# Token division of a memory-augmented attention layer: sums as rows, inverted behind the memory's, spread through DRAM, outputs divided on GpSimd one segment later

## The chip, the cores and the metric

The kernel runs on one core of a Trainium2 chip. The metric is device time in microseconds for one launch; the kernel before takes 1630.69 us (median of 3 runs, 1630.55 to 1631.75). The engines are TensorE (PE; PEld is its weight load), VectorE (DVE), ScalarE (ACT), GpSimd (POOL) and SyncE (SP), which issues most DMAs. GpSimd cannot read PSUM, the memory that matmuls write to.

## What is computed

The input is 2048 rows of 512. Two layers alternate, twice: A, B, A, B, each added to its input after a layer norm. The change is in A, attention with a recurrent memory:

```python
for s in range(n_seg):                       # 64 segments of 32 tokens
    h = concatenate([mem, x[segment s]])     # 8 memory rows + 32 tokens
    q, k, v = h @ Wq, h @ Wk, h @ Wv         # 32 heads of 128
    p = softmax(where(mask, q @ k.T * scale, -1e9))
    o = (p @ v) @ Wo
    mem = o[:8]                              # goes into the next segment
    outs.append(o[8:])
```

The mask lets every row see the memory and each token the tokens up to itself. Only `mem` passes from segment to segment. B is a gated MLP over all rows (projection, gelu, layer norm, a 2048 x 2048 matmul across tokens, product, output projection).

## The kernel before, in words

All weights stay in SBUF. Each of the two A blocks runs 64 calls of `segment` (L891); `s` is the segment, `tb` a block of four segments (128 tokens), `j4` its number in the block. TensorE, VectorE and ScalarE run in the order of the program; GpSimd's and SP's order is chosen by the scheduler.

A segment computes Wo for the memory rows of its own segment together with the first 24 tokens of the segment before, so that 32 columns are full: `uT_cur` holds both, and the last 8 tokens of each segment (`oB`) are multiplied with Wo much later, in groups of four blocks (`y_part`). The order on TensorE is:

1. q and k for both halves of the heads (`qk`, L701: 16 matmuls of 512 columns, four at a time in column tiles; r is the half) and v for r = 0 (`v_mm`). ScalarE casts each result (L908), VectorE transposes it into QQ or KA (L911).
2. `scores(0)`, v for r = 1, `scores(1)`. ScalarE takes the exponent (`exps`, L943), VectorE multiplies by the mask into E (`close`, L946). Between the two `close` VectorE casts v (L1040).
3. `sums_ahead` (L969) gives the memory rows' softmax sums for r = 0; `pv(r)` (L986, L989) gives the unnormalised outputs in PSUM, psO[r]; `sums_memory` (L960) gives the memory rows' sums for r = 1; `sums_tokens` (L978) gives those of the token rows, on all 128 partitions at once because its weights are ones: 1024 numbers per partition in psT.
4. `memory_out(r)`: ScalarE inverts the memory's sums as exp(-ln) (L1003, L1004) and VectorE multiplies psO by them into uT_cur (L1005).
5. `wo_pairs` (L777, heads 0 to 17 into px) and `wo_rest` (L784, heads 18 to 31 into pw). `fold` (L873, L875, with ScalarE's copy `cross`, L1065) and `build_hA` (L882, L883) turn the result into the memory rows of hT, which the next segment's first matmul reads. `store_o` writes the 32 rows out through SP (L889).
6. ScalarE inverts all of psT (L1067, two L1070) into Rt, and VectorE divides the tokens: `tok_out` (L1008) into the next segment's uT, `last_out` (L1011) into oB, for r = 0 and 1.

At three points a `fill()` runs other TensorE work out of a generator: q, k and v of the last 8 tokens of the next blocks (`b_units`, six chunks of 16 matmuls of 0.86 us), or the Wo product of older oB rows (`y_part`). `b_units` hands out a chunk as 4 + 12 or 16 matmuls, so a segment takes 4, 12 and 16 at its three points: around `sums_ahead`, and at the end, while memT is built. Eight segments in all (j4 = 3 of the first four blocks of each A) have none. `run(copies)` casts the chunks on ScalarE; SP transposes them by DMA (L767). GpSimd copies, for a coming segment, the parts of QQ (L864) and KX (L867) that belong to other segments' last tokens (`prep_segment`).

Of the kernel before, what the change touches and what calls it, by code (L numbers as in the profile page):

```python
# [53 lines left out]
def _consts(ctx, tc, c, b_sp):  # L54
    nc = tc.nc
    cp = ctx.enter_context(tc.tile_pool(name="consts", bufs=1))
    bsp = cp.tile([P, 16], F32, name="bsp")
    tctx = ExitStack()
    tmp = tctx.enter_context(tc.tile_pool(name="consts_tmp", bufs=1))
    ident_f = tmp.tile([P, P], F32, name="ident_f")  # L60
    nc.gpsimd.memset(ident_f[:], 0.0)
    nc.gpsimd.affine_select(out=ident_f[:], in_=ident_f[:], compare_op=ALU.not_equal, fill=1.0,
                            base=0, pattern=[[-1, P]], channel_multiplier=1)
    ident_bf = cp.tile([P, P], BF16, name="ident_bf")
    nc.vector.tensor_copy(ident_bf[:], ident_f[:])


    maskf = tmp.tile([P, 224], F32, name="maskf")
    nc.gpsimd.memset(maskf[:], 1.0)
    fourth = tmp.tile([P, 4, 32], F32, name="fourth")  # L70
    nc.gpsimd.memset(fourth[:], 0.0)
    nc.gpsimd.affine_select(out=fourth[:], in_=fourth[:], compare_op=ALU.not_equal, fill=1.0,
                            base=0, pattern=[[-1, 4], [-4, 32]], channel_multiplier=1)
    own = maskf[:, 160:224].rearrange("p (i q) -> p i q", i=4)
    is_own = tmp.tile([P, 4, 1], F32, name="is_own")
    nc.vector.tensor_reduce(out=is_own[:], in_=fourth[:], op=ALU.max, axis=mybir.AxisListType.X)
    nc.vector.tensor_copy(own, is_own[:].to_broadcast([P, 4, 16]))
    for q in range(0, P, 32):
        blk = maskf[q:q + 32, 0:160].rearrange("p (i q) -> p i q", i=4)[:, :, 8:32]
        nc.gpsimd.affine_select(out=blk, in_=blk, compare_op=ALU.is_ge, fill=0.0, base=8,  # L80
                                pattern=[[0, 4], [1, 24]], channel_multiplier=-1)
        last = own[q:q + 32, :, 8:16]
        nc.gpsimd.affine_select(out=last, in_=last, compare_op=ALU.is_ge, fill=0.0, base=0,
                                pattern=[[1, 4], [4, 8]], channel_multiplier=-1)
    maskN = cp.tile([P, 2, 224], BF16, name="maskN")
    nc.vector.memset(maskN[:], 0.0)
    for gs in range(4):
        nc.vector.tensor_copy(maskN[32 * gs:32 * gs + 32, gs % 2, :], maskf[32 * gs:32 * gs + 32, :])
    ones = cp.tile([P, P], BF16, name="ones")
    nc.vector.memset(ones[:], 1.0)  # L90
    half = cp.tile([P, 2, 32], BF16, name="half")
    nc.vector.memset(half[:], 0.0)
    for g in range(2):
        nc.vector.memset(half[64 * g:64 * g + 64, g, :], 1.0)
    bsp_bf = cp.tile([P, 16], BF16, name="bsp_bf")

    def load_bsp():
        nc.vector.memset(bsp_bf[:], 0.0)
        nc.sync.dma_start(bsp_bf[:], b_sp.rearrange("(t p) -> p t", p=P))
        return lambda: nc.vector.tensor_copy(bsp[:], bsp_bf[:])  # L100

    c["bsp"], c["load_bsp"] = bsp, load_bsp
    tctx.close()
    c.update(ident_bf=ident_bf, maskN=maskN, ones=ones, half=half)
    return c


# [374 lines left out]
def kernel(  # L482
# [30 lines left out]
    rp = ctx.enter_context(tc.tile_pool(name="rows", bufs=1))  # L513
    rows = _Rows(nc, rp, xd, xb_d, o_d, x_in)
    rows.vb_d = dram.tile([P, 8 * DH], BF16, name="vb_d")
    with tc.manual_schedule(engines=ORDERED):
        _act_table(nc)
        for tt in range(2):
            x = rp.tile([P, DM], F32, name="x0", tag=("ln_x", "y_x")[tt])[:, 0:DM // 2].bitcast(BF16)
            nc.sync.dma_start(x, x_in[tt * P:(tt + 1) * P, :])  # L520
            rows.xs[tt] = x
        m0 = rp.tile([2 * M, DM], BF16, name="m0", tag="y_o")
        nc.vector.memset(m0[:], 0.0)
        nc.sync.dma_start(m0[0:M, :], A_mem0.rearrange("b m d -> (b m) d"))
        rows.m0T = rp.tile([P, KT, 2 * M], BF16, name="m0T")
        nc.sync.dma_start_transpose(out=rows.m0T[:], in_=m0[:].rearrange("t (kt s) -> t kt s", s=P))
        wqkv, rest = a_open_qkv_weights(tc, ctx, A_Wq, A_Wk, A_Wv)
        c = {}
        _ln_consts(ctx, tc, c)
        MV, RS = c["MV"], c["RS"]  # L530
        for tt in range(2):
            _stats(nc, rp, rows.xs[tt], MV[0][:, tt, :])
            _rstd_act(nc, RS[0][:, tt:tt + 1], MV[0][:, tt, 1:2], c)
            rows.apply(tt, MV[0], RS[0], first=True)
        _consts(ctx, tc, c, B_b_sp)
        rest()
# [120 lines left out]
def a_block(tc, c, rows, front, MV_in, RS_in, MV_out, RS_out, ahead, wo, S, first):  # L657
# [1 line left out]
    NSEG = S // SEG  # L659
    NB = S // P  # L660
    scale = float(DH) ** -0.5
    maskN, ones, half = c["maskN"], c["ones"], c["half"]

    with ExitStack() as ctx:

# [10 lines left out]
            KTBr[i], QTBr[i] = (a.rearrange("p (r h k) -> p r h k", r=2, h=16) for a in v[2:])  # L676
        pers = ctx.enter_context(tc.tile_pool(name="a_pers", bufs=1))
        wk = ctx.enter_context(tc.tile_pool(name="a_work", bufs=2))
        vsp = ctx.enter_context(tc.tile_pool(name="a_vs", bufs=2))
        rowp = ctx.enter_context(tc.tile_pool(name="a_rows", bufs=4))  # L680
        segp = ctx.enter_context(tc.tile_pool(name="a_seg", bufs=2))
        acc_pool = ctx.enter_context(tc.tile_pool(name="a_ps_acc", bufs=1, space=PSUM))
# [26 lines left out]

        memT = [pers.tile([P, P], BF16, name=f"memT{i}") for i in range(2)]  # L710
        NKQ = 2
        KAr = [pers.tile([P, 2, 16, 32], BF16, name=f"KA{i}") for i in range(2)]
        QQr = [pers.tile([P, 2, 16, 40], BF16, name=f"QQ{i}") for i in range(NKQ)]
        KXr = [pers.tile([P, 4, 2, 32], BF16, name=f"KX{i}") for i in range(NKQ)]
        uT = [pers.tile([P, H, 32], BF16, name=f"uT{i}") for i in range(2)]
# [20 lines left out]
        def run(todo):  # L736
            while todo:
                todo.pop(0)()

        def b_units(tb, early=0):  # L740
# [3 lines left out]
            for k, j in enumerate(order):  # L744
                now = k < early
                ps = (accB if now and k % 2 and j != 5 else accA).tile([P, 512], F32, name="psb")[:]
                for kts in (((0,), (1, 2, 3)), ((0, 1, 2, 3),))[k % 2]:
                    mm_chunk(ps, lambda kt, cg: bs["hB"][:, kt, :],
                             lambda kt, cg: qk_rhs(w, j, kt, cg) if j < 4 and now else cols_rhs(w, j, kt, cg), kts)
                    if kts[-1] != KT - 1:  # L750
                        yield
# [48 lines left out]
        def y_part(G, q, last=False):  # L800
# [5 lines left out]
                parts = [[(groups[g], 8 * q + k) for g in range(4)] for k in range(8)]  # L806
            pwB = accA.tile([P, DM], F32, name="pwB")
            for k, _ in enumerate(wo_last(parts, pwB)):
                if k in (0, 3):
                    yield  # L810

            def add(lo, n, src):
# [43 lines left out]

        seg_state = {}
        oBs = {}

        def prep_segment(s, eng=nc.gpsimd):  # L860
            tb, j4 = s // 4, s % 4
# [29 lines left out]
        def segment(s, fill, spare1, spare2, spare3, tail, loads):  # L891
            tb, j4 = s // 4, s % 4
            st = seg_state.pop(s)
            QQ, KX, VX = st["QQ"], st["KX"], st["VX"]
            KA = KAr[s % 2]
            VA = vsp.tile([P, 2, 4, DH], BF16, name="VA")
            hA_cur = rows.hT[tb][:, :, 24 + 32 * j4:56 + 32 * j4]
            uT_cur, uT_nxt = uT[s % 2], uT[(s + 1) % 2]
# [73 lines left out]
            def sums_tokens(ps):  # L972

                for k in range(2):
                    for g in range(2):
# [2 lines left out]
                        nc.tensor.matmul(o[:, :, :, 24:32] if k else o, lhsT=ones[64 * g:64 * g + 64, :],  # L978
                                         rhs=e_own(e, 1) if k else e_all(e, 8, 40), start=(k == 0), stop=True, skip_group_check=True)

            def pv(r):

                for i in range(4):
# [17 lines left out]
            def memory_out(r, ps):  # L1001
                rm = Rm[:, r]
                nc.scalar.activation(out=rm, in_=ps, func=ACT.Ln)  # L1003
                nc.scalar.activation(out=rm, in_=rm, func=ACT.Exp, scale=-1.0)  # L1004
                nc.vector.tensor_tensor(out=hview(uT_cur[:], r, 24, 32), in0=oview(r, 0, 8), in1=rm.rearrange("p g (n q) -> p g n q", q=8), op=ALU.mult)  # L1005

            def tok_out(r):
                nc.vector.tensor_tensor(out=hview(uT_nxt[:], r, 0, 24), in0=oview(r, 8, 32), in1=rview(r, 0, 24), op=ALU.mult)  # L1008
# [45 lines left out]
            spare1(E)  # L1054
            pv(1)
            sums_memory(1, sums[1])
            sums_tokens(psT)
            memory_out(1, sums[1])
            run(copies)
            px = accB.tile([P, 512], F32, name="px")  # L1060
            wo_pairs(px, uT_cur)
# [1 line left out]
            wo_rest(pw, uT_cur)  # L1063
            cross = wk.tile([P, P], F32, name="cross", bufs=1)
            beside = nc.scalar.copy(cross[0:64, :], px[64:128, 128:256])  # L1065
            Rt = segp.tile([P, 2, 512], F32, name="Rt", tag="Rt", bufs=1)
            nc.scalar.activation(out=Rt[:], in_=psT[:], func=ACT.Ln)  # L1067
            for r in range(2):
                rt = Rt[:, :, 256 * r:256 * r + 256]
                nc.scalar.activation(out=rt, in_=rt, func=ACT.Exp, scale=-1.0)  # L1070
            run(turns)
            spare2()
            t1 = wk.tile([P, P], F32, name="t1", bufs=1)
# [3 lines left out]
            if s > 0:  # L1077
                store_o(s, pw, t1)
            spare3()
            tok_out(0)  # L1080
            last_out(0)
            fill()
            run(copies)
            tok_out(1)
            last_out(1)
            run(adds)
            run(turns)
            tail()
# [4 lines left out]
        if first:  # L1093
            for tb in range(2):
                ln_turn(tb, nc.scalar.copy)
            units, units1 = b_units(0, 6), b_units(1, 2)
            for gen in (units, units1, units):
                for _ in range(3):
                    next(gen)
                    run(turns)  # L1100
                    run(copies)
                run(turns)
        else:
            blk_state[0] = dict(KTB=KTBr[0], QTB=QTBr[0], VB=VBr[0], VX=wo.VX[0])
# [7 lines left out]
            rows.y_load(y, first, nc.gpsimd, rows.pool.tile([P, DM], F32, name="y_x")[:], o)()  # L1112

        def values(units):
            for n in (2, 1):
                for _ in range(n):
                    next(units)
                run(copies)
                yield
# [151 lines left out]
```

## Time and profile before

| | us |
|---|---|
| median of 3 runs | 1630.69 |
| the profiled execution: its span | 1630.2 |
| a usual segment, from its first psQ matmul to the next one's | 10.00 |
| the first A block's segments 0 to 63 start at | 33.0 to 680.2 |
| the second A block's segments start at | 839.4 to 1475.0 |
| granted TensorE clock, mean | 0.996 |

The profiled execution has no run time of its own beside its span; the span is 0.5 us under the median of the runs. The page gives for each engine its busy time and share; a group's line gives code line, engine, operation, tile written <- tiles read, shapes, count, busy time, mean ns of one, and the idle time before it with what ended it. A matmul group's duration in a timeline runs to its modelled end; the distance to the next start is what it costs TensorE. The two A blocks hold some 1310 us of the span (33 to 693 and 839 to 1489), B nearly all of the rest.

### The profile page before, as it was taken

What the parts mean: (1) busy time and instruction counts of PE and PEld (TensorE: products, weight loads), DVE (VectorE), ACT (ScalarE), POOL (GpSimd) and SP (SyncE); (2) the same over time, 40 slices, a digit from 0 to 9 for tenths busy, and PEclk for the clock granted to TensorE, in tenths of its full rate; (3) what the DMA queues carried; (4) which work ended last, traced back from release to release, by engine and by line L of the source; (5) the groups of instructions that cost most, each with busy time, mean ns of one, the idle gap of its engine ahead of it and who ended that gap; (6) DMA issues with size and microseconds to landing.
All of it is one profiled execution on the core that took longest, in us unless ns stands there. A gap on an engine that the chain in (4) does not pass through costs nothing.

```text
span 1630.2 us, 90461 instructions
## 1 busy us (share of the span) xinstructions
PE 1575.0 (97%) x40658; PEld 962.0 (59%) x40658; DVE 1211.3 (74%) x3179; ACT 1064.1 (65%) x2278; POOL 290.2 (18%) x604
## 2 busy tenths in 40 slices
PE   4899999999999999999999999999999999999999
PEld 1456665665566556566656566666655666664565
DVE  3677777778888888884467777777888788878622
ACT  2577777777777777661047777777777777775400
POOL 5111111111211221320011111111121112224000
PEclk9899999999999999999999999999999999999999
DMA  9322122223321334387951222121233123425697
GB/s 352 105 44 43 44 44 44 43 46 75 81 56 43 79 87 84 91 182 145 214 167 48 45 50 46 46 46 46 62 97 79 46 72 95 98 55 172 141 189 162
DMA packets 264748, 149.27 MB, mean 92 GB/s; under 512 B 198680, under 2 KB 240784, under 8 KB 264360
## 3 DMA queue, kind: packets, MB, share of 16 engines
q1 hardware_dynamic: 251128, 99.66, 28.4%
q0 software_dynamic: 13232, 43.82, 8.3%
q8 instruction: 319, 5.23, 1.4%
q14 instruction: 69, 0.57, 0.1%
HBM read 59.68 MB, written 37.19 MB: 59 GB/s over the span
## 4 chain that ended last, share of the span: by engine, by line
PE 54%; DVE 1%; ACT 1%; DMA 1%; issue 0%; SPq 0%; DVEq 0%
PE pg L392 9%; PE psQ L701 7%; PE psK L701 7%; PE psb L701 5%; PE pz L291 4%; PE px L777 4%; PE psV L701 3%; PE psm L701 3%; PE psO L784 3%; PE py L435 2%; PE psO L986 2%; PE pwB L796 1%; PE psT L978 1%; PE psS L934 1%; PE pw L1223 0%; PE psO L969 0%
## 5 line engine op out<-in xcount | busy, mean ns | idle before, releaser
L701 PEld LDWEIGHTS <-hT 128*32 128x32 bf16 x12288 | 331.9, 97 | 309.2 <-DVE hT L883 65.5
L911 DVE STREAM_TRANSPOSE QQ<-rows 128x512 bf16<-128x512 bf16 x256 | 179.2, 700 | 20.2 <-ACT rows L908 13.0
L911 DVE STREAM_TRANSPOSE KA<-rows 128x512 bf16<-128x512 bf16 x256 | 176.3, 689 | 14.7 <-ACT rows L908 13.1
L908 ACT CAST rows<-psQ 128x512 bf16<-128x512 f32 x256 | 142.8, 584 | 22.7 <-PE psQ L701 21.1
L392 PE MATMUL pg<-z,wspT 128*128 128x344 bf16 x1024 | 154.3, 309 | 0.0
L1005 DVE TENSOR_TENSOR uT<-psO,Rm 128x128 bf16<-128x128 f32 x256 | 74.5, 291 | 106.7 <-PE psO L989 56.6
L1070 ACT ACTIVATE Rt<-Rt 128x512 f32<-128x512 f32 x256 | 147.3, 622 | 4.1
L1008 DVE TENSOR_TENSOR uT<-psO,Rt 128x384 bf16<-128x384 f32 x256 | 140.4, 548 | 10.8 <-ACT Rt L1070 4.1
L701 PE MATMUL psQ<-Wq_sb,hT 128*32 128x512 bf16 x2048 | 136.2, 383 | 10.2 <-ACT Rt L1067 4.4
L943 ACT ACTIVATE S<-psS 128x224 bf16<-128x224 f32 x256 | 91.4, 357 | 81.1 <-PE psS L938 81.1
L777 PEld LDWEIGHTS <-uT 128*32 128x32 bf16 x4608 | 111.6, 96 | 46.8 <-DVE uT L1005 32.7
L701 PE MATMUL psQ<-Wk_sb,hT 128*32 128x512 bf16 x2048 | 136.2, 383 | 0.0
L777 PE MATMUL px<-Wo,uT 128*32 128x256 bf16 x3840 | 135.3, 275 | 0.3 <-DVE uT L1005 0.3
L701 PE MATMUL psm<-Wq_sb,hT 128*32 128x512 bf16 x2048 | 134.9, 380 | 0.0
L701 PE MATMUL psK<-Wk_sb,hT 128*32 128x512 bf16 x2048 | 134.4, 379 | 0.0
L701 PE MATMUL psK<-Wv_sb,hT 128*32 128x512 bf16 x2048 | 134.4, 379 | 0.0
L701 PE MATMUL psV<-Wv_sb,hT 128*32 128x512 bf16 x2048 | 133.6, 378 | 0.0
L1067 ACT ACTIVATE Rt<-psT 128x1024 f32<-128x1024 f32 x128 | 131.0, 1024 | 3.1
L784 PE MATMUL psO<-Wo_high,uT 128*32 128x128 bf16 x7168 | 126.9, 220 | 5.9 <-issue 3.3
L392 PEld LDWEIGHTS <-wspT 128*128 128x128 bf16 x1024 | 100.2, 98 | 53.2
L867 POOL COPY KX<-old 128x128 bf16<-128x128 bf16 x128 | 69.1, 550 | 299.3 <-PE psS L938 224.8
L867 POOL COPY KX<-front 128x128 bf16<-128x128 bf16 x126 | 66.6, 548 | 303.9 <-PE psS L938 222.5
(194 smaller groups left out, 2908.2 us busy)
## 6 DMA issues: line engine op xcount, KB each, us to landing
o_d<-o_sb SPq DMA_DIRECT2D x126, 64.0 KB
vb_d<-front SPq DMA_DIRECT2D x30, 256.0 KB
VX<-vb_d SPq DMA_DIRECT2D x120, 64.0 KB
ln_x<-xd SPq DMA_DIRECT2D x26, 256.0 KB
y_o<-o_d POOLq DMA_DIRECT2D x22, 256.0 KB, 3.4
xd<-y_o POOLq DMA_DIRECT2D x22, 256.0 KB, 3.2
Wq_sb<-in_A_Wq_dram POOLq DMA_DIRECT2D x8, 512.0 KB, 9.7
Wk_sb<-in_A_Wk_dram POOLq DMA_DIRECT2D x8, 512.0 KB, 11.1
```

The source lines that it names most:

```text
L392: nc.tensor.matmul(pg[t][:, k, 0:344], lhsT=wsp[t][:, st, :], rhs=z(st, 344 * k, 344 * k + 344), start=(st == 0), stop=(st == NT - 1))
L701: return [nc.tensor.matmul(ps[32 * cg:32 * cg + 32, :], lhsT=lhs(kt, cg), rhs=rhs(kt, cg), start=(kt == 0), stop=(kt == KT - 1), tile_posi ...
L777: nc.tensor.matmul(px[at:at + 32, 0:256], lhsT=lhs[:, h, :], rhs=wo_rhs(h, slice(k + 2, None, -2) if h % 2 else slice(k, None, 2)), start= ...
L784: nc.tensor.matmul(pw[32 * cg:32 * cg + 32, :], lhsT=lhs[:, h, :], rhs=wo_rhs(h, cg), start=False, stop=(h == H - 1), tile_position=(0, 32 ...
L867: eng.tensor_copy(KX[:, :, r].rearrange("p g (k i) -> p i g k", i=4), bs["KTB"][:, r].rearrange("p (i g) k -> p i g k", i=4)[:, :, :, 8 * ...
L908: return r, mms, nc.scalar.copy(r[:], ps)
L911: nc.vector.transpose(out=QQ[:, j % 2, :, 0:32] if j < 2 else KA[:, j % 2], in_=r[:])
L943: return nc.scalar.activation(out=S[:, r], in_=psS[:, r, 0:224], func=ACT.Exp, scale=scale)
L1005: nc.vector.tensor_tensor(out=hview(uT_cur[:], r, 24, 32), in0=oview(r, 0, 8), in1=rm.rearrange("p g (n q) -> p g n q", q=8), op=ALU.mult)
L1008: nc.vector.tensor_tensor(out=hview(uT_nxt[:], r, 0, 24), in0=oview(r, 8, 32), in1=rview(r, 0, 24), op=ALU.mult)
L1067: nc.scalar.activation(out=Rt[:], in_=psT[:], func=ACT.Ln)
L1070: nc.scalar.activation(out=rt, in_=rt, func=ACT.Exp, scale=-1.0)
```

## The change

`sums_rows` replaces `sums_tokens` in all segments but the last of each A. Its weights, `pick`, put the sums of 64 partitions on 16 equal rows, so that eight matmuls of at most 128 columns give all sums as 8 distinct rows, psT[:, 0, 0:128], instead of 1024 numbers on each partition. Right behind the memory's inversion ScalarE inverts these 128x128 numbers (Rr). SP writes the 8 distinct rows to DRAM (`r_d`, 4 KB) and reads them back four times with all 128 partitions as the target (Rt, 4 x 128 KB). The unnormalised outputs leave PSUM as copies into `raw` (f32): r = 1 by ScalarE behind `cross`, r = 0 by VectorE where `tok_out(0)` stood. Four GpSimd products of `raw` and Rt fill uT and oB; they are emitted in the next segment, behind its `sums_rows`. A fourth `fill()` stands ahead of the memory's second inversion, between the sums and `wo_pairs`, and the chunks are handed out as 4 + 8 + 4 and 16 matmuls. KA and VA become single buffers.

```diff
+    pick = cp.tile([P, 2, 16], BF16, name="pick")
+    nc.vector.memset(pick[:], 0.0)
+    for g in range(2):
+        nc.vector.memset(pick[64 * g:64 * g + 64, g, :], 1.0)
...
+    rows.r_d = [dram.tile([8, P], F32, name=f"r_d{i}") for i in range(2)]
...
-        vsp = ctx.enter_context(tc.tile_pool(name="a_vs", bufs=2))
+        vsp = ctx.enter_context(tc.tile_pool(name="a_vs", bufs=1))
...
-        KAr = [pers.tile([P, 2, 16, 32], BF16, name=f"KA{i}") for i in range(2)]
+        KAr = [pers.tile([P, 2, 16, 32], BF16, name="KA")]
...
-                for kts in (((0,), (1, 2, 3)), ((0, 1, 2, 3),))[k % 2]:
+                for kts in (((0,), (1, 2), (3,)), ((0, 1, 2, 3),))[k % 2]:
...
-                if k in (0, 3):
+                if k in (0, 2, 3):
                     yield
...
+            def sums_rows(ps):
+
+                for k in range(2):
+                    for q in range(4):
+                        e = E[:, q // 2, q % 2, :]
+                        rhs = e[:, 160:224].rearrange("p (i b e) -> p i b e", i=4, b=2)[:, :, 1, :] if k else heads40(e[:, 0:160])[:, :, 8:40]
+                        o = ps[32 * q:32 * q + 32, :].rearrange("p (i q) -> p i q", i=4)
+                        nc.tensor.matmul(o[:, :, 24:32] if k else o, lhsT=pick[:].rearrange("p g m -> p (g m)"), rhs=rhs,
+                                         start=(k == 0), stop=True, tile_position=(0, 32 * q), skip_group_check=True)
...
+            def raw_out(raw, r, copy):
+
+                copy(raw[:].rearrange("p (r g n) q -> p r g n q", r=2, g=2)[:, r], oview(r, 8, 40))
...
             sums_memory(1, sums[1])
-            sums_tokens(psT)
+            ahead_of = s + 1 < NSEG
+            if ahead_of:
+                sums_rows(psT[:, 0, 0:P])
+            else:
+                sums_tokens(psT)
+            if late:
+                late.pop(0)()
+            if not (first and s == 0):
+                fill()
             memory_out(1, sums[1])
+            Rt = segp.tile([P, 2, 512], F32, name="Rt", tag="Rt", bufs=1)
+            if ahead_of:
+                Rr = segp.tile([P, P], F32, name="Rr", bufs=1)
+                nc.scalar.activation(out=Rr[:], in_=psT[:, 0, 0:P], func=ACT.Ln)
+                nc.scalar.activation(out=Rr[:], in_=Rr[:], func=ACT.Exp, scale=-1.0)
+                r_d = rows.r_d[s % 2]
+                nc.sync.dma_start(r_d[:], Rr[:].rearrange("(a b) c -> a b c", b=16)[:, 0, :])
+                for q in range(4):
+                    nc.sync.dma_start(Rt[:, q // 2, :].rearrange("p (g s c) -> p g s c", g=2, s=2)[:, :, q % 2, :],
+                                      r_d[2 * q:2 * q + 2, :].partition_broadcast(P))
             run(copies)
...
-            nc.scalar.activation(out=Rt[:], in_=psT[:], func=ACT.Ln)
-            for r in range(2):
-                rt = Rt[:, :, 256 * r:256 * r + 256]
-                nc.scalar.activation(out=rt, in_=rt, func=ACT.Exp, scale=-1.0)
+            if ahead_of:
+                raw = segp.tile([P, H, 32], F32, name="raw", bufs=1)
+                raw_out(raw, 1, nc.scalar.copy)
+
+                def norm_tokens():
+
+                    rb = Rt[:].rearrange("p r (h q) -> p (r h) q", q=32)
+                    for o, lo, hi in ((uT_nxt[:, :, 0:24], 0, 24), (oB[:, :, 8 * (s % 16):8 * (s % 16) + 8], 24, 32)):
+                        for r in range(2):
+                            n = slice(16 * r, 16 * r + 16)
+                            nc.gpsimd.tensor_tensor(out=o[:, n], in0=raw[:, n, lo:hi], in1=rb[:, n, lo:hi], op=ALU.mult)
+
+                late.append(norm_tokens)
+            else:
...
-            tok_out(0)
-            last_out(0)
+            if ahead_of:
+                raw_out(raw, 0, nc.vector.tensor_copy)
+            else:
+                tok_out(0)
+                last_out(0)
             fill()
             run(copies)
-            tok_out(1)
-            last_out(1)
+            if not ahead_of:
+                tok_out(1)
+                last_out(1)
```

The last segment of each A keeps the old path. The start of the first A and its first segment hand out four parts in place of three.

## Prediction, on record before the run

> **What bounds the kernel now.** I read the page's shares, then the windows of single segments, then the timeline of one segment, then the DMA and GpSimd queues. Times inside a segment are counted from its first psQ matmul and written T+.
>
> ```profile
> PE 1575.0 (97%) x40658; PEld 962.0 (59%) x40658; DVE 1211.3 (74%) x3179; ACT 1064.1 (65%) x2278; POOL 290.2 (18%) x604
> ```
>
> TensorE looks full, but that does not say that its work sets the time. From one segment's first psQ matmul to the next one's, most of the 128 segments take 10.00 us, and a few take 9.80. The windows of one of each (length, then busy us and instructions of PE, PEld, DVE, ACT and POOL, granted clock, DMA share, GB/s):
>
> ```profile
> 1041.22:1051.22 10.00, 10.00 (x309) 5.99 (x308) 7.93 (x21) 7.55 (x17) 1.80 (x4) 1.00 0.15 38
> 910.90:920.70 9.80, 8.76 (x277) 5.36 (x273) 8.10 (x21) 7.28 (x17) 2.39 (x5) 1.00 0.20 43
> ```
>
> The second has no `fill` in it: 1.72 us less TensorE work (32 matmuls, 0.86 us per 16) buys only 0.20 us. So a chain through all engines takes 9.80 us, and a filled segment is 0.20 us of TensorE work above it. The end of that chain, in the unfilled segment:
>
> ```profile
> 917.05 0.38 DVE L946 TENSOR_TENSOR E<-S,maskN 128x448 bf16<-128x448 bf16 x1
> ...
> 917.49 0.32 PE L986 MATMUL psO<-E,VA 64*128 64x80 bf16 x8 [0.41 <-ACT Rm L1004]
> ...
> 917.70 0.22 PE L960 MATMUL psO<-E,ones 64*128 64x64 bf16 x4
> ...
> 917.75 0.44 PE L978 MATMUL psT<-E,ones 64*128 64x512 bf16 x4
> ...
> 917.99 0.28 ACT L1003 ACTIVATE Rm<-psO 128x128 f32<-128x128 f32 x1 [0.49 <-PE psO L960]
> ...
> 918.12 1.05 PE L777 MATMUL px<-Wo,uT 128*32 128x256 bf16 x30
> ...
> 918.64 0.29 DVE L1005 TENSOR_TENSOR uT<-psO,Rm 128x128 bf16<-128x128 f32 x1 [0.36 <-ACT Rm L1004]
> ...
> 918.90 0.39 PE L777 MATMUL px<-Wo_high,uT 128*32 128x256 bf16 x6
> ```
>
> The second E (E1, L946) ends at T+6.53, its pv at once follows, then the memory's sums, Ln, Exp, the product for heads 16 to 31 (done T+8.03), heads 16 and 17 of px, the rest, fold, memT, hT. L978, which the change removes, stands beside this chain: Ln starts without it, and heads 0 to 15 (32 matmuls, 0.85 us) end at T+8.07, just when the chain delivers.
>
> **What the change takes away.** TensorE loses L978's step (917.75 to 918.12, 0.37) and gets eight matmuls of 32 columns; sixteen such (L969) step 0.12, so 0.06 to 0.12, say 0.10. A quarter chunk of fill (0.215) moves from ahead of pv to ahead of px. A filled segment is then bound by the chain up to heads 16 (T+8.09), four more matmuls (0.11), the rest of Wo (step 0.78), and the last fill (0.86): 9.85. An unfilled one stays at 9.80, which is why I count nothing for TensorE there. 126 segments change, 8 are unfilled: 118 x 0.15 = **17.7 us**.
>
> VectorE drops two 0.55 (L1008) and two 0.28 (L1011) for one PSUM copy like L1040's 0.69. It lies after memT, beside the next segment's projections; the transposes behind it are then released by TensorE. Only segments now over 10.00 can gain; all their excess is 10.7 us, and I take 2.
>
> ScalarE drops 1.02 + 2 x 0.62 of Rt and gets Ln 0.28 and Exp 0.31 on 128x128 and one raw copy (0.58). The Ln and Exp now stand ahead of the chunk's cast and `cross`: after L1004 (start T+7.39) starts step 0.22, 0.31, 0.22, 0.51, so cross starts at T+8.65 instead of T+8.44. L875 then ends at T+9.23, while pw's last matmul lands at T+9.16: 0.01 to 0.05 late, inside the 9.85. If the cast took longer, each tenth would be on the chain.
>
> Sum so far: 1630.2 - 17.7 - 2 = **1610.5**.
>
> **What it adds: the division on GpSimd.** Per segment four products of two SBUF operands, 128x384 twice and 128x128 twice. The nearest row is L223 on GpSimd, 128x512 f32, 1.21; scaled 0.91, so 0.93. The floor is 0.60 (L864, 256 elements copied in 0.40, times 1.5), the ceiling 1.21. The small ones lie between hB's 0.30 and KX's 0.55: 0.42. The four take 2.7 us. GpSimd has 8 us spare per segment, so its sum costs nothing; its place does. The product for segment s is built into GpSimd's queue ahead of the KX and QQ copies that wait for the next scores, so it runs as soon as its Rt halves have landed.
>
> When is that? Exp of Rr ends at T+8.23. SP writes r_d; the nearest landings in the trace's events are o_d<-o_sb (64 KB, median 2.43, fastest 2.38) and xb_d (fastest 1.71, median 2.92): I take 2.1 for 4 KB. Only then do the four Rt loads go out, at the 0.45 spacing of VX's issues. A VX load of 64 KB lands in 1.8 to 3.6, median 2.87, behind a 256 KB write; for 128 KB with little ahead I take 2.4. The first half is there at 8.27 + 2.1 + 0.05 + 0.45 + 2.4 + 0.05 = 13.3, which is **T+3.5** of the next segment; the ends (1.7 and 1.8; 3.2 and 3.6) give T+2.5 to T+5.8. The second half follows 0.9 later. Where hT's transpose (1.20) and ln_x (0.58) are ahead of r_d on SP, which is every fourth segment, it is 1 us later. px needs the products at T+7.2 and T+8.1: they are done by T+5.8, so TensorE does not wait for GpSimd.
>
> By the Trainium skill, "DMA: Bandwidth & Descriptors", section "Anatomy of one DMA — SWDGE (gpsimd) path", a DMA costs about 2.0 us plus bytes over 436 GB/s; that is given for the other queue, and an estimate by it (2.0 and 2.3) puts the first half at T+3.3 and the sum at about 1657. The medians of the rows above are higher, so the trace does not agree.
>
> But the products then run exactly where VectorE multiplies S by the mask: E0 asks at T+5.12 and E1 at T+6.14, with VectorE's 0.69 cast between them without a gap. These two exclude GpSimd. In the trace a KX copy that begins 0.02 to 0.03 after E takes 0.685 instead of 0.477, and an E that begins just after a GpSimd copy takes longer by the copy's size: 0.49 behind 128 elements, 0.61 behind 256, against 0.38 alone. The second case and its GpSimd copies, from the timelines:
>
> ```profile
> 1127.63 0.61 DVE L946 TENSOR_TENSOR E<-S,maskN 128x448 bf16<-128x448 bf16 x1
> ```
>
> ```profile
> 1127.60 0.40 POOL L864 COPY QQ<-old 128x256 bf16<-128x256 bf16 x1 [0.81 <-PE psO L969]
> 1127.94 0.62 POOL L867 COPY KX<-old 128x128 bf16<-128x128 bf16 x1
> ```
>
> The block is about 0.9 ns per copied element; a product reads twice as much and takes 0.93, so I let it hold VectorE for 0.85. With the first half at T+3.5: products 3.50 to 4.43, 4.85, then the second large one 4.85 to 5.78; E0 asks at 5.12, runs at 5.70, 0.58 late, E1 and the chain as much. The delay is a sawtooth in the arrival: worked the same way, T+3.0, 3.25, 3.5, 3.75 and 4.0 give 0.10, 0.35, 0.60, 0.85 and 0.28, mean 0.44. Arrivals will scatter as the landings do; I take 0.40. 126 x 0.40 = **50 us**. The floor is nothing (arrival by T+2.5, or hits in a gap), the ceiling about 0.65 (the mean around T+4.4).
>
> The Trainium skill, "SBUF — State Buffer", section "SBUF: two separate sides", speaks against the change too: a VectorE operation with two SBUF inputs and a reading GpSimd operation lock each other out "for the whole instruction". The trace agrees that they exclude, not on the length: behind the whole 0.40 of QQ the E above would have taken 0.75, it took 0.61. An estimate by the rule makes each block some 0.1 longer and the sum about 1670.
>
> Sum: 1610.5 + 50 = 1660.5. The profiled span of 1630.2 stands 0.5 below the median of the runs, 1630.69, so **1661**.
>
> **The rest at nothing.** The Rt loads write 0.5 MB more per segment, 1024 packets of 512 B at the 29 ns of such packets, 1.9 us on 16 engines out of 10: hidden by engines that are 15 to 21% busy, else landings move later. SP's issues add 0.4 + 4 x 0.45 and a wait of 2; behind them stand o_d (its tile is rewritten 6 us later) and K's transposes (used a segment later). Single KA and VA buffers are rewritten at T+2.7 and T+5.0, after their readers of the segment before.
>
> **Rivals.**
> - *Faster, 1610 (0.26).* The products miss E: Rt lands by T+2.5, or a product holds VectorE much shorter than a copy's 0.9 ns per element lets expect. For it: the fastest landings just give that. Against: the medians, and the transposes in the same queue.
> - *No change, 1630 (0.08).* Hits cost 0.16 on average and eat the gain, or the cast on ScalarE does.
> - *Much slower, 1750 (0.04).* Landings of 4 us put the products behind T+6; px then waits for GpSimd. At T+6.0 the E delay is 0.7 and px waits 0.4: 126 x 1.1 on 1610.
> - That the scheduler queues this segment's KX copies behind the products, so that scores wait, is excluded by the built order: those copies serve the segment after next.
> - *My forecast, slower around 1661 (0.62),* its own range 1636 to 1690, turned by one mechanism: E behind a product on the shared port. It decides at a mean delay of 0.16.
>
> **How the numbers follow.** Faster 0.26; same 0.08; slower 0.62 + 0.04. A difference within 0.2% (1627.4 to 1634) cannot be told from none here. The range reaches from the fast rival, 1606, to the ceiling of 0.65 per segment, 1692.
>
> **What would show it.** Right: E's spans of 0.4 to 1.2 us with GpSimd products beside them; TensorE's idle time ended by E ahead of the second pv; filled segments of 10.1 to 10.6 us; the products starting at T+3 to T+4.5. Wrong: E at 0.39 throughout and filled segments at 9.85 (fast rival), or px's weights waiting for GpSimd's uT (late rival), or cross waiting for nothing but ScalarE with L875 the last to arrive (no change).

## The result, and the profile after

The changed kernel takes 1765.8 us (median of 4 runs, 1757.8 to 1774.0) against 1630.6 for the kernel before: 1.082 times as long, 95% interval 1.0774 to 1.0866. I had forecast 1661 and a range up to 1692: the change did lose, but by more than four times as much. The profiled execution has a span of 1770.0 us.

The page after, engines, then two of the DMA queues (packets, MB, share of 16 engines' span) and the chain that ended last:

```profile
PE 1612.5 (91%) x41139; PEld 981.4 (55%) x41162; DVE 1191.7 (67%) x2804; ACT 953.8 (54%) x2278; POOL 630.2 (36%) x1108
...
q1 hardware_dynamic: 390232, 166.27, 41.7%
...
q8 instruction: 323, 5.29, 1.3%
...
PE 65%; DMA 13%; DVE 9%; POOL 3%; issue 3%; ACT 3%; SPq 2%; POOLq 0%; DVEq 0%; ACTq 0%
```

The shares of PE, DVE and ACT all fell: the time has grown, and DVE and ACT have less work, part of which went to GpSimd (630.2 us busy, 290.2 before). Before, the chain was TensorE, with 1% of DMA and 1% of VectorE in it; now 13% is DMA and 9% VectorE. q1 carried 99.7 MB before (28.4%); what came on top, 66.6 MB, is the 126 writes of r_d with their Rt loads. q8 brings instructions, in packets of 16 KB (5.23 MB before); it will matter.

A segment takes 11.27 us on average in the first A and 11.03 in the second (10.08 and 10.07 before; the first two segments of each A are left out), about 1.1 us more in some 125 segments. Two of them show two ways to lose. Windows of both (length, busy us of the engines, clock, DMA):

```profile
1044.44:1054.95 10.51, 10.04 (x309) 5.97 (x309) 7.46 (x18) 6.44 (x16) 4.31 (x8) 1.00 0.34 87
999.92:1011.98 12.06, 10.26 (x310) 5.96 (x313) 7.04 (x18) 6.44 (x16) 4.10 (x8) 1.00 0.28 78
```

In the first, a product meets E (timeline):

```profile
1050.30 0.99 POOL L1114 TENSOR_TENSOR uT<-raw,Rt 128x384 bf16<-128x384 f32 x1 [5.43 <-DMA Rt<-r_d]
...
1050.59 0.95 DVE L952 TENSOR_TENSOR E<-S,maskN 128x448 bf16<-128x448 bf16 x1
...
1051.60 0.32 PE L1002 MATMUL psO<-E,VA 64*128 64x80 bf16 x8 [0.47 <-DVE E L952]
```

E takes 0.95 in place of 0.39 and the second pv waits for it, as forecast; but the product starts at T+5.9, not T+3.5. In the second segment Rt is later still. Its SP queue and GpSimd's products:

```profile
997.90 1.19 SPq L209 DMA_TRANSPOSE hT<-ln_xn  x1
999.14 0.57 SPq L198 DMA_DIRECT2D ln_x<-xd  x1
999.82 0.59 SPq L1093 DMA_DIRECT2D r_d<-Rr  x1
```

```profile
1003.20 2.89 SPq L1095 DMA_DIRECT2D Rt<-r_d  x4
...
1007.81 0.98 POOL L1114 TENSOR_TENSOR uT<-raw,Rt 128x384 bf16<-128x384 f32 x1 [5.57 <-DMA Rt<-r_d]
...
1008.85 1.05 PE L782 MATMUL px<-Wo,uT 128*32 128x256 bf16 x30 [1.50 <-POOL uT L1114]
...
1010.21 0.29 PE L782 MATMUL px<-Wo_high,uT 128*32 128x256 bf16 x4 [0.31 <-POOL uT L1114]
```

The write of r_d is issued behind hT and ln_x, 0.1 us before the segment starts, the loads follow 3.4 us later, the product runs at T+7.9, and px, for which TensorE stood idle from T+7.4, at T+8.9. E is undisturbed here. A third kind of loss has no partner in the segment at all: TensorE waits for nothing that the profile shows. The waits of TensorE's weight loads (us in total, times, longest):

```profile
PEld L782 <- POOL uT L1114: 56.6, 58, 5.1
PEld L1002 <- ACT Rm L1019: 48.2, 114, 0.4
PEld L1002 <- DVE E L952: 41.2, 75, 2.9
...
PEld L706 <- issue: 34.9, 81, 3.0
...
PEld L975 <- issue: 29.9, 52, 2.9
```

The wait for Rm (L1019) was there before (50.5). "issue" of all TensorE lines sums to 96.5 us of weight-load waits, 27.7 before.

### The profile page after: what moved, and what is told of

It is laid out like the page before. It is cut to its first block, busy times and chain, and to the rows that moved or that the text cites. A ratio compares the mean times of both kernels' runs of the same rounds, so it can differ in the third digit from the quotient of the medians.

```text
span 1770.0 us, 92820 instructions
## 1 busy us (share of the span) xinstructions
PE 1612.5 (91%) x41139; PEld 981.4 (55%) x41162; DVE 1191.7 (67%) x2804; ACT 953.8 (54%) x2278; POOL 630.2 (36%) x1108
## 4 chain that ended last, share of the span: by engine, by line
PE 65%; DMA 13%; DVE 9%; POOL 3%; issue 3%; ACT 3%; SPq 2%; POOLq 0%; DVEq 0%; ACTq 0%
PE psQ L706 11%; PE psK L706 10%; PE pg L396 8%; PE psb L706 6%; DMA Rt<-r_d 6%; PE px L782 5%; DVE E L952 5%; PE psO L789 5%; PE psm L706 5%; PE pz L295 4%; DMA r_d<-Rr 3%; POOL uT L1114 2%; PE psO L1002 2%; PE py L439 2%; DVE VA L1060 2%
## 5 line engine op out<-in xcount | busy, mean ns | idle before, releaser
L706 PEld LDWEIGHTS <-hT 128*32 128x32 bf16 x12288 | 336.1, 97 | 325.8 <-DVE hT L889 70.8
L1114 POOL TENSOR_TENSOR uT<-raw,Rt 128x384 bf16<-128x384 f32 x252 | 254.9, 1011 | 664.2 <-DMA Rt<-r_d 506.9
L914 ACT CAST rows<-psQ 128x512 bf16<-128x512 f32 x256 | 149.7, 585 | 137.6 <-PE psQ L706 137.6
L917 DVE STREAM_TRANSPOSE KA<-rows 128x512 bf16<-128x512 bf16 x256 | 181.8, 710 | 40.8 <-ACT rows L914 34.9
L782 PEld LDWEIGHTS <-uT 128*32 128x32 bf16 x4608 | 123.1, 97 | 86.4 <-POOL uT L1114 56.6
L952 DVE TENSOR_TENSOR E<-S,maskN 128x448 bf16<-128x448 bf16 x256 | 159.3, 622 | 15.2 <-POOL seen L1197 0.6
L706 PE MATMUL psQ<-Wq_sb,hT 128*32 128x512 bf16 x2048 | 140.5, 385 | 19.5 <-DVE hT L889 10.9
L789 PE MATMUL psO<-Wo_high,uT 128*32 128x128 bf16 x7168 | 133.4, 225 | 8.8 <-issue 6.7
L1019 ACT ACTIVATE Rm<-psO 128x128 f32<-128x128 f32 x256 | 71.1, 278 | 112.9 <-PE psO L966 92.2
L789 PEld LDWEIGHTS <-uT 128*32 128x32 bf16 x7168 | 120.0, 100 | 12.7 <-issue 11.7
L706 PE MATMUL psb<-Wq_sb,hB 128*32 128x512 bf16 x992 | 87.1, 391 | 21.3 <-ACT hB L629 16.8
```

Source lines behind the costliest of these rows:

```text
L706: return [nc.tensor.matmul(ps[32 * cg:32 * cg + 32, :], lhsT=lhs(kt, cg), rhs=rhs(kt, cg), start=(kt == 0), stop=(kt == KT - 1), tile_posi ...
L782: nc.tensor.matmul(px[at:at + 32, 0:256], lhsT=lhs[:, h, :], rhs=wo_rhs(h, slice(k + 2, None, -2) if h % 2 else slice(k, None, 2)), start= ...
L789: nc.tensor.matmul(pw[32 * cg:32 * cg + 32, :], lhsT=lhs[:, h, :], rhs=wo_rhs(h, cg), start=False, stop=(h == H - 1), tile_position=(0, 32 ...
L914: return r, mms, nc.scalar.copy(r[:], ps)
L917: nc.vector.transpose(out=QQ[:, j % 2, :, 0:32] if j < 2 else KA[:, j % 2], in_=r[:])
L952: nc.vector.tensor_tensor(out=E[:, r], in0=S[:, r].unsqueeze(1).to_broadcast([P, 2, 224]), in1=maskN[:], op=ALU.mult)
```

## The experiments

Theories at the start: **lateness** (the trips through DRAM end later than I reckoned; products meet E, and px waits), **traffic** (the transfers or SP's queue delay other work), **rearrangement** (the new order itself loses). The times, each with its ratio to runs of the kernel before on the same chip (four chips; the kernel before takes 1629.2 to 1630.9 on them); the last column sums the weight-load waits named issue:

| run | us | ratio, 95% interval | issue |
|---|---|---|---|
| before | 1630.6 | | 27.7 |
| no_trip | 1639.0 | 1.0031 to 1.0068 | 41.5 |
| cross_first | 1638.4 | 1.0039 to 1.0070 | 43.6 |
| trip_small | 1631.2 | 0.9998 to 1.0024 | 32.0 |
| trip_alone | 1683.8 | 1.0315 to 1.0367 | 75.9 |
| short_products | 1712.5 | 1.0475 to 1.0528 | 82.7 |
| changed kernel | 1765.8 | 1.0774 to 1.0866 | 96.5 |
| before_half | 1637.1 | 1.0030 to 1.0065 | 35.2 |
| before_one | 1655.6 | 1.0106 to 1.0183 | 52.1 |
| before_trip | 1674.8 | 1.0244 to 1.0298 | 68.4 |
| products_on_E | 1643.5 | 1.0056 to 1.0098 | |
| on_E | 1694.8 | 1.0370 to 1.0434 | 34.0 |
| behind_E | 1898.3 | 1.1571 to 1.1690 | 34.4 |
| one_load | 1722.9 | 1.0537 to 1.0606 | 86.8 |
| half_bytes | 1731.4 | 1.0598 to 1.0671 | 85.6 |
| one_load_ord | 1766.8 | 1.0815 to 1.0860 | 92.8 |
| half_bytes_ord | 1728.6 | 1.0558 to 1.0624 | 76.9 |

**The trip taken out, alone, and small.** no_trip drops the five DMAs:

```diff
-                nc.sync.dma_start(r_d[:], ...)
-                for q in range(4):
-                    nc.sync.dma_start(Rt[...], r_d[2 * q:2 * q + 2, :].partition_broadcast(P))
```

> Leaves out the write of r_d and the four Rt loads; Rt is filled once with ones, so the token outputs stay undivided. Lateness theory (the two trips through DRAM end later than I reckoned, so that the products meet E and px waits for them): nothing of the loss is left, products start before T+2, E takes 0.39, 1605 to 1620 us. Traffic theory (the transfers and SP's queue delay other work): the same, 1605 to 1620. Rearrangement theory (Rr's inversion ahead of cross, the sums as rows, the fourth fill, single KA and VA lose time themselves): still over 1640.

1639: nearly the whole loss is gone, but nothing is gained either; of that below. trip_alone keeps the DMAs and takes the products out:

```diff
-                            nc.gpsimd.tensor_tensor(out=o[:, n], in0=raw[:, n, lo:hi], in1=rb[:, n, lo:hi], op=ALU.mult)
+                            if lo:
+                                nc.gpsimd.memset(o[:, n], 0.5)
+                            else:
+                                nc.gpsimd.tensor_tensor(out=junk[:, n], in0=raw[:, n, 0], in1=rb[:, n, 0], op=ALU.mult)
```

> The write of r_d and the Rt loads stay, but the products of uT shrink to 16 elements per partition into a tile that nothing reads, and those of oB become a constant, so the token outputs are wrong. Nothing waits for Rt but GpSimd, and nothing long stands beside E. Lateness theory: 1605 to 1630 us, E at 0.39. Traffic theory: over 1700, as slow as the changed kernel or nearly. Rearrangement theory: over 1640.

1684: not what lateness gives, and less than I had given traffic. It stands 45 us above no_trip, which still has the long products, although no engine but GpSimd waits for Rt directly. trip_small tells whether SP's issues or the packets do this (its short products, too, cover 2 partitions only):

```diff
-                    nc.sync.dma_start(Rt[:, q // 2, :]..., r_d[2 * q:2 * q + 2, :].partition_broadcast(P))
+                    nc.sync.dma_start(Rt[0:2, q // 2, :]..., r_d[2 * q:2 * q + 2, :].partition_broadcast(2))
```

> As the run with the trip alone (nothing waits for Rt, no long products, token outputs wrong), but the four Rt loads fill 2 partitions in place of 128: the same five issues on SP and the same waits there, 1/64 of the bytes and packets. Traffic theory (the 1024 packets of the Rt loads keep the DMA engines from bringing TensorE's next block of instructions in time): the waits named issue fall back to some 50 us, 1635 to 1650 us. If SP's issues and its wait for r_d do the harm: 1675 to 1690.

1631: the packets. Where the 53 us between the two runs lie, weight-load and matmul waits of trip_small, then of trip_alone (their line numbers are one higher behind L721: L789 is L790):

```profile
PEld L706 <- issue: 14.1, 39, 2.9
PEld L790 <- issue: 10.1, 21, 2.1
PE psO L790 <- issue: 4.6, 13, 0.9
PEld L783 <- issue: 3.6, 2, 2.9
```

```profile
PEld L706 <- issue: 28.2, 53, 2.9
PEld L790 <- issue: 26.2, 36, 2.1
PE psO L790 <- issue: 18.1, 31, 1.7
PEld L783 <- issue: 13.4, 19, 2.9
```

Each grew twofold or more; all waits of weight loads named issue grew by 44 us. Beside them TensorE's matmuls wait 14 us more for hT and uT, and VectorE waited 18.7 us for loads of y_o that GpSimd issues (0.5 in trip_small); half_bytes below shows how.

The trace's DMA records say what the waits named issue are: in trip_alone 82 of the 127 (53.7 of 75.9 us) end 1.2 to 1.8 us behind the end of a q8 packet, in trip_small 32 of 75 (11.9 us), in the kernel before 18 of 63 (8.1 us); ends that fell at random would be there in 12%. So, by their timing, these are waits for the next block of instructions. Where the Rt loads hold it up is not shown: the packet itself takes no longer (median 0.98 us, 1.13 before). In the 3 us before the 82 packets start there are some 670 packets of 512 B, against 380 before any packet of q8; in before_trip, below, that difference is small (395 against 370). The Trainium skill, "Runtime: NRT & Kernel Launch", section "Instruction fetch mechanics", says that instructions are streamed in 16 KiB blocks of 256 and that this is mostly hidden. The packets of q8 have that size, and an estimate by it gives TensorE's 41139 matmuls and 41162 weight loads 321 blocks, where q8 has 322 packets in trip_alone. Hidden it is not beside loads like these.

**The same traffic in the kernel before.** To see it without the change, r_d is written from Rm and loaded into a tile that nobody reads:

```diff
+                nc.sync.dma_start(r_d[:], Rm[0:8, 0].rearrange("p g n -> p (g n)"))
+                for q in range(4):
+                    nc.sync.dma_start(junk[...], r_d[2 * q:2 * q + 2, :].partition_broadcast(P))
```

> The kernel before, with only the traffic of the change added: in each segment SP writes 4 KB of Rm to r_d and reads it back with four loads of 128 KB into a tile that nobody reads (KA and VA are single, to make room for it). Nothing waits for it and GpSimd does nothing more. Traffic theory (the loads delay TensorE's instruction blocks, whatever the kernel's order): 1670 to 1685 us, waits named issue some 100 us. If only the changed order of work is sensitive to the loads: 1630 to 1640.

> As the run with the trip added to the kernel before, but the 512 KB of a segment come in one DMA of 128 packets of 4 KB in place of four of 1024 packets of 512 B. If the time for which the loads hold the DMA engines delays TensorE's instruction blocks (q1's share was the same for both forms): 1670 to 1680 us as with four loads. If the number of packets or of loads does it: 1635 to 1655.

> As that, with 256 KB in one DMA of 128 packets of 2 KB. If bytes count: half of the 45 us, 1645 to 1658. If one load costs what it costs whatever its size: as the run with 512 KB.

45, 25 and 6 us over the kernel before on the same chips. The waits named issue rise by 41 (to 68, where I had expected some 100), 24 and 8: they are nearly all of the loss. Of these waits 35.4, 32.1 and 12.4 us end 1.2 to 1.8 us behind a q8 packet, 8.1 in the kernel before. KA and VA are single in all three, so that costs 6 us at most. Both the packets (512 KB in 1024 or in 128 packets: 45 or 25) and the bytes (512 or 256 KB in 128 packets: 25 or 6) count, so my alternatives were too simple: q1's share is 45.5%, 43.5% and 36.4%.

**Lateness without long products.** short_products is trip_alone with the 16 elements per partition going into uT, so px waits for Rt:

> As the run with the trip alone, but the 16 elements per partition go into uT, so that px still waits for Rt; the token outputs are wrong. Lateness theory: E's part of the loss (61 us of E above 0.385) is gone, TensorE's waits in the segments where Rt comes after T+7 stay: 1670 to 1720 us. If the port alone made the loss: 1605 to 1630. Traffic theory: over 1740.

1712.5, inside the band: 29 us are px waiting for Rt (weight loads waited 35.5 us for uT, 38 times).

**The port.** products_on_E copied an element of S into a scratch tile ahead of the products, without the trip. Nothing bound the products to that copy, the scheduler put them ahead of it, and of the 252 large ones only 14 started between T+3.5 and T+9; so it answers nothing.

> No transfer at all (Rt filled once with ones, outputs undivided), but the products wait for the first exponent, so that they start together with the first E, at about T+5.1, in every segment. Lateness theory, its part on the shared port: E is 0.85 to 1.0 late in each segment although nothing is moved by DMA, px does not wait for uT: 1690 to 1760 us. If it is the Rt loads writing into SBUF that slow E, and not the products: 1605 to 1630.

on_E writes the elements into uT, where the products must follow:

```diff
+                nc.gpsimd.tensor_copy(uT_cur[:, 0:17:16, 0:1], S[:, 0, 0:2].unsqueeze(2))
                 late.pop(0)()
```

> As the run with products meant to start on E, but now bound to it: a copy of two elements of the first exponent goes into uT ahead of the products. No transfers (Rt is ones, outputs undivided). Port theory (a product with two SBUF inputs and E exclude each other, and that is the 53 us between the changed kernel and the run with short products): E is 0.4 to 0.85 late in each segment, 1690 to 1746 us from the 1639 without the trip. If the port costs little and those 53 us are something else: 1640 to 1660.

1694.8, 56 us over no_trip, with no DMA added. Most segments take 10.31. One of them, from 1043.55:

```profile
1049.21 2.10 POOL L1113 TENSOR_TENSOR uT<-raw,Rt 128x384 bf16<-128x384 f32 x2
1049.71 0.75 DVE L952 TENSOR_TENSOR E<-S,maskN 128x448 bf16<-128x448 bf16 x1
...
1050.52 0.32 PE L1002 MATMUL psO<-E,VA 64*128 64x80 bf16 x8 [0.27 <-DVE E L952]
```

The second E asks while the first product (1.00 of the 2.10 us) runs, and ends 0.25 us behind it. So products alone, with no Rt loads, hold E up: by 0.36, just under the 0.4 that I had expected at least. The usual segment takes 0.37 more than in no_trip, an estimated 45 of the 56 us over 125 segments; beside that px's weights waited 28.9 us for uT in 37 cases, and this run does not separate the two. behind_E binds the products of the whole changed kernel to the second E in the same way:

> The whole changed kernel, with the products held until the second E is done (two elements of it are copied into uT first). Port theory: E is back at 0.39, but the large products now end at T+7.6 and T+8.6 where px asks at T+7.3 and T+8.0, so each segment pays about 0.6 for px on top of the 1684 of the trip alone: 1750 to 1790 us, the loss moves from E to px. If E's delay was the greater evil: 1700 to 1730.

1898, far above. Weight loads of px waited

```profile
PEld L782 <- POOL uT L1115: 245.4, 228, 8.8
```

four times as long as in the changed kernel. Part is what I had reckoned (undisturbed segments take 10.75). The rest: GpSimd ran the two small products, which were not held, and copies for QQ and KX ahead of the held ones, so that in late segments these too stand between Rt and px (in the segment from 1148.12, Rt is there at T+7.0, the first large product starts at T+9.4); and TensorE's clock was granted at half for 133 us in all, against 58 in the changed kernel and 14 before. One thing speaks against a fixed price of the loads: behind_E moves the same bytes, and its waits named issue sum to 34.4 us only. Whether the long waits for uT give the blocks time to arrive is not tested.

**Better trips.** one_load brings Rt in one DMA of 4 KB packets, half_bytes the same in bf16; the two runs named ord have GpSimd in the order of the program:

```diff
-                    nc.sync.dma_start(Rt[:, q // 2, :]..., r_d[2 * q:2 * q + 2, :].partition_broadcast(P))
+                nc.sync.dma_start(Rt[:].rearrange("p r e -> p (r e)"), r_d[:].rearrange("a c -> (a c)").partition_broadcast(P))
```

> The changed kernel with Rt loaded by one DMA of 128 packets of 4 KB in place of four with 1024 packets of 512 B; r_d stays in the order of its rows, and the products are eight of 192 or 64 elements per partition. The computation is whole. Lateness and traffic theories: Rt is there about 1.5 us earlier and occupies the DMA engines for less time, fewer late instruction blocks, px seldom waits for uT: 1690 to 1735 us. If bytes alone count and the arrival does not matter: 1750 to 1780.

> As the run with one load, but Rr leaves ScalarE as bf16 and r_d and Rt are bf16: one DMA of 128 packets of 2 KB, 256 KB per segment in place of 512. The computation is whole. Traffic theory (what costs is the time in which the loads hold the DMA engines): half of the 45 to 53 us of the trip alone goes, and Rt is there 0.5 to 1 us earlier: 1680 to 1700 us from 1723. If the number of trips and not their size counts: 1715 to 1730.

> The run with one load, with GpSimd's instructions in the order of the program, so that the loads of older outputs stand ahead of the products that wait for Rt. There VectorE had not waited for those loads: nothing changes, 1710 to 1730 us. If the scheduler's order of GpSimd mattered in other ways too: under 1700.

> The run with half the bytes, with GpSimd's instructions in the order of the program. If the 8 us by which it was slower came of VectorE's 40 us of waits for the loads of older outputs: those waits go and the time falls to 1685 to 1700 us. If bytes do not count: 1715 to 1730 as the run with one load in this order.

One load saves 43 us. Not all of that is the transfer: the products are split in two (0.59 us in place of 1.00 each), and with them E's time above 0.385 falls from 61 to 30 us, while px's weights wait 31.5 us for uT in place of 56.6 and the waits named issue only fall from 96.5 to 86.8. No run separates these. Half the bytes saved nothing on top; the waits of VectorE in half_bytes hold

```profile
DVE y_o L237 <- DMA y_o<-o_d: 40.0, 12, 4.7
```

which one_load does not have: GpSimd, which issues that load, stood at a product that waited for Rt. In program order this wait is gone (0.3 us), but the time is not: 1728.6 where I had expected 1685 to 1700. So that wait does not explain alone why half the bytes saved nothing. That order is itself slower by 44 us with one load, against my expectation: weight loads wait 65.4 us for uT, 31.5 in one_load. Within it half the bytes save 38 us (1728.6 against 1766.8). Which instruction ahead of the products makes the order slow is not settled.

**Where the gain went.** cross_first is no_trip with Rr's Ln and Exp moved behind `cross`:

> As the run without the trip (Rt is ones, outputs undivided), but ScalarE's Ln and Exp of Rr stand behind cross in place of ahead of it. If cross, which ends at T+8.95 there and so lets t1 end at T+9.28, is what holds filled segments at 9.94: most of them take 9.85 and the time falls by 8 to 12 us, to 1620 to 1630. If something else holds them: 1631 to 1640 as before.

The time stayed, though `cross` did hold the filled segments a little. no_trip (segment from 906.67) and cross_first (from 902.25):

```profile
915.36 0.26 ACT L1101 COPY cross<-px 64x128 f32<-64x128 f32 x1
...
915.65 0.29 DVE L881 TENSOR_TENSOR t<-px,cross 128x128 f32<-128x128 f32 x1 [0.23 <-ACT cross L1101]
```

```profile
910.71 0.26 ACT L1097 COPY cross<-px 64x128 f32<-64x128 f32 x1 [0.31 <-PE px L782]
...
911.10 0.29 DVE L881 TENSOR_TENSOR t<-px,cross 128x128 f32<-128x128 f32 x1
```

L881 starts at T+8.98 in the one, held by `cross`, and at T+8.85 in the other; undisturbed filled segments take 9.94 and 9.88. But the mean over the segments is 10.09 and 10.10, as before (10.07): issue waits of 41.5 and 43.6 us in place of 27.7 can have taken back what the shorter usual segment gives (0.06 and 0.12 in 118 segments, 7 and 14 us). That is a sum and not a test: trip_small has 32.0 us of such waits, and its filled segments take mostly 10.05 or 9.94. In any case no version on this path that I ran beats the kernel before, not even with a division that needs no trip. Deferring the products by one more segment was not tried.

## Why the prediction was wrong

- **"The rest at nothing": wrong, the largest term that I had left out.** "Hidden by engines that are 15 to 21% busy" looked at the engines' mean share and at the transfers that I had listed, not at q8. TensorE waits for its instruction blocks beside the loads, and these cost 53 us (trip_alone against trip_small), 45 in the kernel before.
- **"When is that?": wrong.** From r_d's issue to the first half of Rt I had 5.0 us; the trace has 6.6 (10 to 90%: 5.7 to 7.8). The write lands in 1.67 (I took 2.1), but an Rt load takes 3.6 where I took 2.4, four follow each other at 0.47 and more, and in a quarter of the segments SP issues r_d 0.9 us or more behind Exp, which itself ends at T+8.65 in the median and not at T+8.23. The first product starts at T+5.0 in the median, not T+3.5.
- **"They are done by T+5.8, so TensorE does not wait for GpSimd": the step that failed with it.** The last large product ends at T+8.1 in the median. px's wait costs 29 us with short products, more with long ones. My late rival had this mechanism, and a total of 1750, at a chance of 0.04; I had tied it to landings of 4 us, and 3.6 with a queue in front sufficed. That its total lies so near the measured one is luck in part: it had no term for the instruction blocks.
- **E behind the product: right, and near in size.** E's time above 0.385 sums to 61 us (forecast 50), though the products came 1.5 us later than in my sawtooth, so the size is luck in part. Long products in place of short ones cost 53, E and px together. The length I assumed for the block was wrong: E ends 0.25 us behind the product's end, and alone it takes 0.39, so a product excludes it to its end, and only the first 0.14 of E runs beside it. My E of 0.61 behind a QQ copy fits too: the copy ends at 1128.00, E at 1128.24. So the rule of the Trainium skill, "SBUF — State Buffer", section "SBUF: two separate sides", "for the whole instruction", holds, and the trace had agreed with it.
- **The gain of 17.7: not there.** Filled segments came to 9.94, since `cross` sits on the chain by 0.06 to 0.09 where I had it just inside, and issue waits that I had not counted can have taken the rest.
- Along the runs: 1631 (trip_small), +53 traffic, +29 px waiting for Rt, +53 long products: 1766. Each term is the difference of two runs, so they must add up; in another order they might split otherwise. Against my 1661 the gain that did not come is 21, the traffic 53, px 29 and the long products 3.

## What to carry to other kernels

A transfer that nobody waits for need not be free: here it delayed TensorE's instructions. Look for the instruction queue among the DMA queues and for waits named issue, and weigh packets and bytes. A trip through DRAM of two dependent DMAs is write, landing, issues, landing and the queue ahead of both, and its spread, not its median, meets an in-order consumer. Before moving work to GpSimd, list VectorE's operations with two SBUF inputs that fall beside it.

## What the runs showed of the hardware

GpSimd instructions that follow each other without a gap can keep VectorE out over several of them. In the changed kernel, GpSimd, then VectorE:

```profile
1319.57 0.58 POOL L223 DMA_DIRECT2D y_o<-o_d  x1
1320.17 1.00 POOL L1114 TENSOR_TENSOR uT<-raw,Rt 128x384 bf16<-128x384 f32 x1
1321.11 0.46 POOL L1114 TENSOR_TENSOR front<-raw,Rt 128x128 bf16<-128x128 f32 x1
1321.51 0.45 POOL L873 COPY KX<-old 128x128 bf16<-128x128 bf16 x1
1321.78 0.40 POOL L870 COPY QQ<-old 128x256 bf16<-128x256 bf16 x1
```

```profile
1319.83 2.59 DVE L952 TENSOR_TENSOR E<-S,maskN 128x448 bf16<-128x448 bf16 x1
```

E begins before the product and still ends 0.24 us behind the QQ copy; nine E of the changed kernel take over 1.2 us.

A wait of TensorE can have an aftermath. In one segment px waits 2.58 us for GpSimd; windows of the stretch with the wait and of the one behind it (the third column from the end is the granted clock):

```profile
1534.77:1537.73 2.96, 0.38 (x14) 0.07 (x11) 1.01 (x4) 1.54 (x5) 1.04 (x2) 1.00 0.40 113
1538.84:1542.25 3.41, 3.16 (x76) 2.23 (x80) 1.72 (x9) 0.85 (x2) 1.66 (x5) 0.53 0.26 67
```

The clock is full in the wait and near half behind it, so 16 matmuls take 1.49 in place of 0.86. The trace has such stretches, of 3.41 us or a multiple: 58 us of half clock in all against 14 before, which by half the difference is an estimated 22 of the 135 us at most, inside the terms above. The Trainium skill, "TensorE: Matmul & The Clock Gate", Part 1, gives a window of about 3.4 us for this. The stretches agree.
